# Hashed attention and two gated layers: the order of the first loads, zero matmuls on TensorE at the start, and new due times

## The chip, the cores and the metric

The kernel runs on one core of one Trainium2 chip. What counts is the time of one execution on the device in microseconds (us), the median of several runs. The five engines work side by side: PE (TensorE, matmuls; its weight loads are PEld), DVE (VectorE), ACT (ScalarE), POOL (GpSimd), and SP (SyncE), which here issues most of the loads. ACT and POOL can issue loads too.

## The reference

The inputs are q, k and v of shape (2, 8, 768, 64). Six projections give each query and each key a bucket, and a query sees only the keys of its own bucket:

```python
q_bits = (np.einsum('bhsd,dk->bhsk', q, proj) > 0)
...
mask = q_bucket[:, :, :, None] == k_bucket[:, :, None, :]
scores = np.where(mask, scale * np.matmul(q, k.transpose(0, 1, 3, 2)), -1e9)
attn = softmax(scores)
x = (attn @ v), heads side by side: 1536 tokens x 512
h = x @ w_in;  x = (h - tanh(h)) @ w_out
g = x @ w_gate;  x = (g * sigmoid(g) * (x @ w_val)) @ w_out2
```

## The kernel before

The work is attention over 8 pairs of heads, then the two layers over three blocks of 512 tokens. A pair has 12 steps: two halves of the queries, two heads (e = 0 and 1), three blocks of 128 queries. A step (`declare_step`) computes the scores on PE (L438, into one of two PSUM tiles `s_t`), their maximum on DVE (L447), the exp on ACT (L449), divides by the sum (L453, L455 and, on POOL, L456), transposes on PE (L467) and copies to SBUF (L473). After each half `declare_pv` multiplies with v in two parts (L493). The mask is built into the score matmuls: `prep` and `prep_first` hash q and k (L405 and L363), take the signs as bits on DVE (L346), turn them to one-hot sums on PE (L340), and write the operands on ACT, POOL and DVE (L305, L307, L316, L320, L331, L334). `prep_first` does so for pair 0, head by head, from its own loads; for later pairs `prep(n)` uses a tile y that holds q and k of both heads, and loads q and k once more in the layout of the operands.

Nothing is put in order by hand. Each piece of work is declared with `op`: the engines that may do it and how long it takes there, what it reads and writes, a due time, and a time `after` which it may begin. `Plan.order` then runs a list scheduler over these figures: whenever an engine is free, it takes the ready piece with the earliest due time. The result is one order of all pieces. The kernel emits the instructions in this order, each on its engine, and on the chip each engine works its own queue off in that order, waiting only for data and buffers. The figures themselves (durations, `lat`, `slow`, `after`) don't exist on the chip. The table `DUE` holds the offsets that make the due times: `qk` for scores, `tr` for transposes, `pv` and `pv2` for the two parts with v, `mx`, `ex`, `nm`, `cp` for a step's other pieces, `alt` for the second engine where two may do a piece.

Of the kernel before, what the change touches and what calls it, by code (L numbers as in the profile page):

```python
# [10 lines left out]
BF16 = mybir.dt.bfloat16  # L11
# [23 lines left out]
PVB = 3  # L35
NGS = 21
LAG = 1


def chunk_keys():  # L40
# [8 lines left out]
def chunks():  # L49
# [7 lines left out]


DUE = dict(
    pace=2.46, t0=10.5, qk=-13.61, mx=-13.71, ex=10.42, rc=-7.09, nm=-4.48, tr=-11.45, cp=-19.4, alt=-0.38,  # L60
    pv=29.1, pv2=16.93, xh=36.08, xl=19.15, hash=-8.93, bits=-88.0, oh=-8.61, ohs=8.26, pk=7.49, he=19.64,
    ki=-17.93, kl=-2.38, ko=-26.19, qi=8.99, ql=35.3, qb=-9.42, qo=17.11,
)


class Plan:
# [13 lines left out]
    def op(self, eng, fn, r=(), w=(), due=0.0, lat=None, late=False, after=0.0):  # L80
        n = len(self.ops)
        deps = set()
        for k in r:
            deps.update(self.writers.get(k, ()))
        for k in w:
            deps.update(self.writers.get(k, ()))
            deps.update(self.readers.get(k, ()))
        for k in r:
            self.readers.setdefault(k, []).append(n)
        for k in w:  # L90
            if k in r:
                self.writers.setdefault(k, []).append(n)
            else:
                self.writers[k] = [n]
                self.readers[k] = []
        deps.discard(n)
        self.ops.append((dict(eng), fn, deps, due, self.LAT if lat is None else lat, late, after))
# [75 lines left out]
def lsh_attention_moe_kernel(ctx: ExitStack, tc: tile.TileContext, qT, kT, vP, proj, cst, wts, out):  # L173
    nc = tc.nc
    eng = {"PE": nc.tensor, "DVE": nc.vector, "ACT": nc.scalar, "POOL": nc.gpsimd, "SP": nc.sync}
    const = ctx.enter_context(tc.tile_pool(name="const", bufs=1))
    plan = Plan()
    op = plan.op

    def tiles(stack, name, n, shape, dtype=F32, **kw):  # L180
        pool = stack.enter_context(tc.tile_pool(name=name + "_p", bufs=n, **kw))
        return [pool.tile(shape, dtype, tag=name, name=name) for _ in range(n)]
# [19 lines left out]
    s_t = tiles(ctx, "s", 2, [128, 2, 512], space=PSUM)  # L202
# [7 lines left out]
    def ring(name, n):  # L210

        c = counts[name] = counts.get(name, -1) + 1
        return name, c % n
# [42 lines left out]
    v_t = tiles(at, "v", 2, [128, NKT, 128])  # L256
# [13 lines left out]
    def due_at(step):  # L270
        return T0 + PACE * step

    def load(n, side, e, slow=0.0):
        src, t, nm = ((qT, ldq_t, "q"), (kT, ldk_t, "k"))[side]
        k = ring("ld" + nm, 2)
        r0 = (2 * n + e) * 64
        due = due_at(12 * (n - 1) + (2, -1)[side] + 3 * e)
        for i in range(2):
            op({("SP", "ACT")[side == 0 and n == 0]: 0.55},
               lambda g, i=i: g.dma_start(out=t[k[1]][64 * i:64 * i + 64, :], in_=src[r0:r0 + 64, :]),  # L280
               w=[k + (i,)], due=due if n else -5, lat=3.0 + slow)
        return t[k[1]], [k + (0,), k + (1,)]
# [56 lines left out]
    def oh_mm(ps, pk, side, half, bt, btk, due):  # L339
        op({"PE": 0.165}, lambda g: g.matmul(out=ps, lhsT=pw[:, 2 * side + half, :], rhs=bt, start=True, stop=True),  # L340
           r=[btk, "pw"], w=[pk], due=due, lat=0.25)

    def bits_of(ps, pk, due):
        k = ring("bits", 2)
        t = bit_t[k[1]]
        op({"DVE": 0.47}, lambda g: g.tensor_scalar(out=t, in0=ps, scalar1=0.0, scalar2=None, op0=ALU.is_gt),  # L346
           r=[pk], w=[k], due=due)
        return t, k

    def prep_first():  # L350

        lds = {}
        for e in range(2):
            for side in (1, 0):
                lds[e, side] = load(0, side, e, slow=0.3 + 0.9 * e)
        for e in range(2):
            r = slice(64 * e, 64 * e + 64)
            due = due_at(3 * e)
            bank, hk = ((h_t[0], ("h", 0)), (x_t[0], ("x", 0)))[e]

            def hash_head(g, bank=bank, e=e, r=r):
                for j in range(4):
                    g.matmul(  # L363
                        out=bank[32 * j:32 * j + 32, 0:TB], lhsT=pj[r, :],
                        rhs=lds[e, j // 2][0][r, (j % 2) * TB:(j % 2 + 1) * TB],
                        start=True, stop=True, tile_position=(64 * e, 32 * j),
                    )

            op({"PE": 1.45}, hash_head, r=["pj", *lds[e, 0][1], *lds[e, 1][1]], w=[hk], due=(-60.0, due_at(0))[e], lat=0.25)
            bt, btk = bits_of(bank[:, 0:TB], hk, (-60.0, due_at(0))[e])  # L370
            if e == 0:
                sk = ring("s", 2)
                where = {
                    (1, 0): (s_t[sk[1]][:, 0, 0:TB], sk + (0,)), (1, 1): (s_t[sk[1]][:, 1, 0:TB], sk + (1,)),
                    (0, 0): (t_t[0][:, 0, 0:TB], ("t", 0)), (0, 1): (t_t[0][:, 1, 0:TB], ("t", 1)),
                }
            else:
                where = {
                    (1, 0): (t_t[0][:, 0, 0:TB], ("t", 0)), (1, 1): (t_t[0][:, 1, 0:TB], ("t", 1)),
                    (0, 0): (h_t[0][:, 0:TB], ("h", 0)), (0, 1): (x_t[0][:, 0:TB], ("x", 0)),  # L380
                }
            for i, (side, half) in enumerate(((0, 0), (1, 0), (1, 1), (0, 1))):
                ps, pk = where[side, half]
                dd = (-40.0, due_at(1))[e] + 0.2 * i if i < 3 else due_at(4 + 3 * e)
                oh_mm(ps, pk, side, half, bt, btk, (-50.0, due_at(0))[e] + 0.2 * i)
                (prep_k if side else prep_q)(0, e, half, *lds[e, side], ps, pk, dd)

    def load_y(n):
        for side, src in ((0, qT), (1, kT)):
            op({"SP": 0.4}, lambda g, side=side, src=src: g.dma_start(  # L390
                out=y_t[0][:, side, :], in_=src[n * 128:(n + 1) * 128, :]
            ), w=[("y", side)], due=due_at(12 * (n - 1) - 5), lat=4.0)

    def prep(n):
        base = due_at(12 * n)
# [79 lines left out]

    def load_v(n):
        k = v_k[n] = ring("v", 2)
        op({"SP": 0.4}, lambda g: g.dma_start(out=v_t[k[1]], in_=vP[n]), w=[k], due=due_at(12 * n - 3), lat=3.5)

    def declare_pv(n, half):  # L480
        b_, p_ = pairs[n]
# [97 lines left out]
    def a2(g, tb, j):  # L579
        d, ps, skk = a_mm(2, g, tb, 2 * j)  # L580
        u, uk, u1 = u_slot()
        u = u[:, 0:MB]
        op({"ACT": 0.61}, lambda e: e.activation(out=u, in_=ps[:, 0, :], func=ACTF.Sigmoid), r=skk, w=[uk] + u1, due=d + 0.3)  # L583

        def both(e):
            e.tensor_tensor(out=u, in0=ps[:, 0, :], in1=u, op=ALU.mult)  # L586
            e.tensor_tensor(out=u, in0=ps[:, 1, :], in1=u, op=ALU.mult)  # L587

        op({"DVE": 1.38}, both, r=skk + [uk], w=[uk], due=d + 0.9)
        split_g((2, g, tb, j), u, [uk], d + 2.3)  # L590
# [74 lines left out]
    warm = const.tile([128, 1], F32, name="warm")  # L665
    op({"POOL": 0.1}, lambda g: g.memset(warm, 0.0), w=["warm"], due=-100)
    op({"ACT": 1.5}, lambda g: g.activation(out=warm, in_=warm, func=ACTF.Exp), r=["warm"], w=["warm"], due=-3)
    prep_first()
    load_v(0)
    for i in range(nst):  # L670
        n, r = divmod(i, 12)
        declare_step(i)
        if r % 6 == 5:
            declare_pv(n, r // 6)
        if r == 11 and n + 1 < len(pairs):
            prep(n + 1)
            load_v(n + 1)
# [3 lines left out]
    units += [(2, g, tb) for g in range(NG2) for tb in range(NMB)]  # L681
    for n, (layer, g, tb) in enumerate(units + [(0, 0, 0)] * LAG):
        if layer == 2 and g == 0:
# [4 lines left out]
        elif layer == 2:  # L688
            for j in range(G2):
                a2(g, tb, j)  # L690
        if n >= LAG:
            layer, g, tb = units[n - LAG]
            b(layer, g, tb, ((0, 2), (2, 1), (3, 1)))
# [69 lines left out]
```

## Time and profile before

| | |
|---|---|
| time, median of 3 runs | 811.65 us (811.37 to 811.76) |
| the profiled execution | 811.49 us, span of its instructions 809.6 us |
| PE busy | 782.6 us, 97% of the span |
| DVE, ACT, POOL busy | 503.8, 336.3, 382.5 us |
| HBM read | 57.04 MB |

The span runs from the first to the last instruction; the time adds what lies around it. The page of the profile gives the busy time of each engine; the views of the trace that are shown below give it by stretch, instruction by instruction, and with what each waited for.

### The profile page before, as it was taken

The numbers are of one execution on the slowest core, as the hardware profiler recorded it, in microseconds if no ns is written. First come the engines' busy times: TensorE is split into PE (matmuls) and PEld (weight loads), VectorE is DVE, ScalarE is ACT, GpSimd is POOL, SyncE is SP. The second block draws the span as 40 slices with busy tenths as digits, with TensorE's granted clock in tenths as the row PEclk, the third lists the DMA queues.
The fourth block names the chain that finished last, engine by engine and source line by source line (L and its number), as shares of the span: only waits on it lengthen the run. The fifth ranks groups of instructions, "written<-read, shape, count | busy, mean of one in ns | idle before, by whom it ended". The sixth has DMA issues, their size and how long they took to land.

```text
span 809.6 us, 10578 instructions
## 1 busy us (share of the span) xinstructions
PE 782.6 (97%) x3900; PEld 616.3 (76%) x3900; DVE 503.8 (62%) x734; ACT 336.3 (42%) x583; POOL 382.5 (47%) x387
## 2 busy tenths in 40 slices
PE   4899999999999999999999999999999999999998
PEld 2666676666667788888888888888888888888886
DVE  5988787887788497655556359273725646343223
ACT  4877777787674433322222233333222312211110
POOL 3877766766465564533534367353422423231110
PEclk9999999999999999999999999999999999999999
DMA  7453242230214144212113022020402121000012
GB/s 219 124 146 95 70 127 89 79 98 1 73 53 135 55 141 139 79 35 95 53 53 104 27 79 79 26 84 30 147 1 79 55 101 58 20 1 1 1 52 104
DMA packets 20003, 60.86 MB, mean 75 GB/s; under 512 B 2768, under 2 KB 2768, under 8 KB 19952
## 3 DMA queue, kind: packets, MB, share of 16 engines
q1 hardware_dynamic: 19440, 59.25, 22.8%
q10 hardware_dynamic: 464, 0.80, 0.4%
q8 instruction: 31, 0.51, 0.3%
q0 software_dynamic: 48, 0.13, 0.1%
q14 instruction: 20, 0.16, 0.1%
HBM read 57.04 MB, written 3.15 MB: 74 GB/s over the span
## 4 chain that ended last, share of the span: by engine, by line
PE 86%; ACT 5%; DVE 3%; POOL 2%; issue 2%; DMA 1%; ACTq 0%; POOLq 0%
PE s L536 40%; PE t L619 14%; PE h L619 7%; PE x L619 7%; PE x L493 6%; PE t L467 6%; PE s L438 5%; ACT p L449 3%; DVE m L447 2%; POOL p L456 1%; DMA q<-in_qT 1%; ACT pt L473 1%; POOL op L307 1%; ACT op L334 0%; DVE xl L501 0%
## 5 line engine op out<-in xcount | busy, mean ns | idle before, releaser
L545 POOL TENSOR_TENSOR op<-p,op 128x512 fp32r<-128x512 f32 x84 | 115.9, 1390 | 182.2 <-ACT op L544 173.7
L536 PE MATMUL s<-xh,wb 128*128 128x512 f32 x528 | 165.5, 389 | 0.0
L536 PE MATMUL s<-xh,wa 128*128 128x512 f32 x432 | 136.4, 390 | 0.0
L536 PEld LDWEIGHTS s<-xh,wb 128*128 128x128 f32 x528 | 99.1, 188 | 20.6
L456 POOL TENSOR_SCALAR p<-p,r 128x768 f32<-128x768 f32 x96 | 95.2, 997 | 30.7 <-DVE r L455 29.5
L447 DVE TENSOR_REDUCE m<-s 128x1 f32<-128x768 f32 x96 | 89.0, 951 | 22.7 <-PE s L438 22.1
L536 PE MATMUL s<-xl,wb 128*128 128x512 f32 x264 | 102.7, 389 | 0.0
L438 PE MATMUL s<-op 128*128 128x384 f32 x384 | 85.9, 358 | 9.5 <-ACT p L449 9.0
L536 PEld LDWEIGHTS s<-xh,wa 128*128 128x128 f32 x432 | 81.1, 188 | 17.4 <-issue 0.6
L244 POOL TENSOR_TENSOR wb<-f,wb 128x512 fp32r<-128x512 f32 x38 | 52.7, 1393 | 84.6 <-ACT wb L242 73.9
L449 ACT ACTIVATE p<-s,m 128x768 f32<-128x768 f32 x96 | 85.8, 897 | 12.5 <-DVE m L447 10.0
L586 DVE TENSOR_TENSOR p<-s,p 128x512 f32<-128x512 f32 x36 | 24.8, 690 | 104.6 <-ACT p L583 104.6
L467 PEld LDWEIGHTS t<-csb,p 128*128 128x128 f32 x576 | 64.8, 141 | 29.4 <-issue 17.1
L467 PE MATMUL t<-csb,p 128*128 128x128 f32 x576 | 80.7, 276 | 4.4 <-ACT pt L473 2.6
L544 ACT ACTIVATE op<-p 128x512 fp32r<-128x512 f32 x84 | 50.7, 628 | 81.8 <-DVE p L587 50.4
L536 PE MATMUL s<-xl,wa 128*128 128x512 f32 x216 | 84.1, 389 | 0.0
L583 ACT ACTIVATE p<-s 128x512 f32<-128x512 f32 x36 | 21.6, 599 | 139.5 <-PE s L536 138.0
L438 PEld LDWEIGHTS s<-op 128*128 128x128 f32 x384 | 65.1, 191 | 18.6 <-ACT p L449 17.2
L233 DVE TENSOR_SCALAR f<-raw 128x512 uint32<-128x512 uint32 x68 | 54.2, 797 | 33.6 <-POOL wb L244 13.4
L236 DVE SCALAR_TENSOR_TENSOR f<-raw,f 128x512 uint32<-128x512 uint32 x68 | 72.3, 1064 | 1.4
L239 DVE SCALAR_TENSOR_TENSOR f<-raw,f 128x512 uint32<-128x512 uint32 x68 | 69.7, 1026 | 1.0
L493 PE MATMUL x<-pt,v 128*64 128x384 f32 x384 | 68.8, 494 | 0.0
(91 smaller groups left out, 1124.4 us busy)
## 6 DMA issues: line engine op xcount, KB each, us to landing
raw<-in_w SPq DMA_DIRECT2D x68, 512.0 KB, 3.3
k<-in_kT SPq DMA_DIRECT2D x32, 192.0 KB, 3.1
q<-in_qT SPq DMA_DIRECT2D x28, 192.0 KB, 3.6
v<-in_v SPq DMA_DIRECT2D x8, 384.0 KB, 3.5
y<-in_qT SPq DMA_DIRECT2D x7, 384.0 KB, 3.1
y<-in_kT SPq DMA_DIRECT2D x7, 384.0 KB, 4.0
out<-acc SPq DMA_DIRECT2D x3, 512.0 KB, 2.8
out<-acc SPq DMA_DIRECT2D x6, 256.0 KB, 2.1
```

The source lines that it names most:

```text
L233: op({"DVE": 0.6}, lambda e: e.tensor_scalar(out=f, in0=hi32, scalar1=3, scalar2=0x3FFFFFF8, op0=ALU.logical_shift_left, op1=ALU.bitwise_a ...
L236: op({"DVE": 0.95}, lambda e: e.scalar_tensor_tensor(out=f, in0=lo32, scalar=29, in1=f, op0=ALU.logical_shift_right, op1=ALU.bitwise_or), ...
L239: op({"DVE": 0.95}, lambda e: e.scalar_tensor_tensor(out=f, in0=hi32, scalar=0xC0000000, in1=f, op0=ALU.bitwise_and, op1=ALU.bitwise_or), ...
L438: g.matmul(out=s[:, kh, 0:TB], lhsT=(b, a)[first][:, q0], rhs=ks[kh][0 if first else 1], start=first, stop=not first,)
L447: op({"DVE": 0.87}, lambda g: g.tensor_reduce(out=m, in_=sv, axis=AX.XY, op=ALU.max, negate=True), r=[sk + (0,), sk + (1,)], w=[mk], due=d ...
L449: op({"ACT": 0.9}, lambda g: g.activation(out=p.rearrange("p (a b) -> p a b", a=2), in_=sv, func=ACTF.Exp, bias=m, accum_out=sm), r=[sk + ...
L456: op({"POOL": 0.95}, lambda g: g.tensor_scalar(out=p, in0=p, scalar1=r, scalar2=1.0, op0=ALU.mult, op1=ALU.mult), r=[pk, rk], w=[pk], due= ...
L467: g.transpose(out=t_t[0][:, kt // 3, c0:c0 + 128], in_=p[:, kt * 128:(kt + 1) * 128], identity=ident)
L493: g.matmul(out=x[r, :], lhsT=v[:, kt, r], rhs=pt_t[ptks[e][1]][:, kt, :], start=(kt == 0), stop=(kt == NKT - 1), tile_position=(0, 64 * e),)
L536: g.matmul(out=ps, lhsT=w[:, wi, kt * 128:(kt + 1) * 128], rhs=(xh_a, xl_a)[xi][:, kt, tb * MB:(tb + 1) * MB], start=(n == 0), stop=(n == ...
L545: op({"POOL": 1.4}, lambda g: g.tensor_tensor(out=lo, in0=src, in1=hi.bitcast(F32), op=ALU.subtract), r=srck + [hk], w=[lk] + l1, due=due ...
L619: e.matmul(out=o, lhsT=l, rhs=r, start=(n == 0), stop=(n == 3 * ng - 1))
```

## The change

Three things change. The loads of y for every pair may begin in the planner's order only after 5.5, v of pair 0 after 8.0 and v of the other pairs after 16.0, and the planner takes the loads of pair 0 to land later (`slow`). A tile `rest` of zeros is written by DVE, and 66 matmuls multiply it with itself (128 x 128 by 128 x 256, bf16) into the first bank of `s_t[1]`; each may begin in the planner's order at a time of its own and is due at 20.0. And all of `DUE` has new values.

```diff
+WARM = 66
...
 DUE = dict(
-    pace=2.46, t0=10.5, qk=-13.61, mx=-13.71, ex=10.42, rc=-7.09, nm=-4.48, tr=-11.45, cp=-19.4, alt=-0.38,
-    pv=29.1, pv2=16.93, xh=36.08, xl=19.15, hash=-8.93, bits=-88.0, oh=-8.61, ohs=8.26, pk=7.49, he=19.64,
-    ki=-17.93, kl=-2.38, ko=-26.19, qi=8.99, ql=35.3, qb=-9.42, qo=17.11,
+    pace=2.4, t0=13.38, qk=4.32, mx=-25.84, ex=12.05, rc=-10.2, nm=-13.2, tr=-26.1, cp=30.59, alt=-14.51,
+    pv=-7.5, pv2=23.62, xh=36.69, xl=-27.55, hash=-12.04, bits=-92.94, oh=-12.35, ohs=5.39, pk=48.56,
+    he=13.11, ki=-7.49, kl=-9.87, ko=-53.97, qi=-5.84, ql=75.72, qb=19.68, qo=7.53,
 )
...
-                lds[e, side] = load(0, side, e, slow=0.3 + 0.9 * e)
+                lds[e, side] = load(0, side, e, slow=0.4 + 1.2 * e)
...
-            ), w=[("y", side)], due=due_at(12 * (n - 1) - 5), lat=4.0)
+            ), w=[("y", side)], due=due_at(12 * (n - 1) - 5), lat=4.0, after=5.5)
...
-        op({"SP": 0.4}, lambda g: g.dma_start(out=v_t[k[1]], in_=vP[n]), w=[k], due=due_at(12 * n - 3), lat=3.5)
+        op({"SP": 0.4}, lambda g: g.dma_start(out=v_t[k[1]], in_=vP[n]), w=[k], due=due_at(12 * n - 3), lat=3.5, after=(8.0, 16.0)[n > 0])
...
+    rest = const.tile([128, 256], BF16, name="rest")
+    op({"DVE": 0.2}, lambda g: g.memset(rest, 0.0), w=["rest"], due=-100)
+    for i in range(WARM):
+        tm = 0.9 + 0.213 * i if i < 18 else 0.9 + 0.213 * 18 + 0.12 * (i - 18)
+        op({"PE": 0.2 if i < 18 else 0.107}, lambda g: g.matmul(
+            out=s_t[1][:, 0, 0:256], lhsT=rest[:, 0:128], rhs=rest, start=True, stop=True,
+        ), r=["rest"], w=[("s", 1, 0)], due=20.0, lat=0.0, after=tm)
     prep_first()
```

## Rows read from the trace of the kernel before

**Rows 1.** The page, part 1: busy time, share of the span, instructions.
```profile
PE 782.6 (97%) x3900; PEld 616.3 (76%) x3900; DVE 503.8 (62%) x734; ACT 336.3 (42%) x583; POOL 382.5 (47%) x387
```
**Rows 2.** Busy time by stretch at the start, and all attention: length, engines, granted clock.
```profile
17.06:36.50 19.44, 15.06 (x91) 10.87 (x92) 17.98 (x34) 17.79 (x35) 16.97 (x25) 1.00 0.51 148
...
14.40:241.50 227.10, 213.12 (x1372) 150.63 (x1371) 187.43 (x370) 173.48 (x331) 153.83 (x214) 1.00 0.30 89
0.00:10.50 10.50, 1.50 (x8) 0.23 (x8) 3.22 (x8) 3.08 (x6) 2.58 (x10) 1.00 0.81 198
10.50:17.06 6.56, 6.49 (x27) 3.52 (x31) 5.36 (x9) 2.39 (x6) 2.61 (x4) 1.00 0.78 259
```
**Rows 3.** The same view: one attention pair in steady state, and the layers.
```profile
158.40:187.20 28.80, 27.56 (x182) 19.41 (x180) 23.00 (x48) 22.48 (x43) 19.58 (x28) 1.00 0.28 83
...
278.00:540.00 262.00, 262.00 (x1158) 216.94 (x1157) 166.30 (x173) 84.05 (x124) 130.30 (x91) 1.00 0.23 75
```
**Rows 4.** The chain of waits, start to 45 us: start us, us, what.
```profile
0.73 2.35 DMA pj<-in_proj
...
3.11 7.36 DMA q<-in_qT
...
10.51 1.50 PE x L363 x8
...
14.09 2.56 PE s L438 x8
...
39.46 1.39 PE s L438 x8
```
**Rows 5.** Timeline of PE: start us, us, instruction, idle before it and its releaser.
```profile
11.95 0.50 PE L340 MATMUL t<-bits,pw 128*128 128x384 bf16 x1
12.24 0.85 PE L340 MATMUL s<-bits,pw 128*128 128x384 bf16 x2
...
16.98 0.85 PE L405 MATMUL h<-y,pj 128*32 128x384 f32 x8
...
21.52 0.45 PE L438 MATMUL s<-op 128*128 128x384 f32 x1 [0.58 <-ACT op L334]
...
25.87 0.97 PE L438 MATMUL s<-op 128*128 128x384 f32 x4 [0.40 <-ACT p L449]
...
36.50 2.16 PE L493 MATMUL x<-pt,v 128*64 128x384 f32 x12
```
**Rows 6.** DMA view of four short stretches: issues with us to landing, bytes, rates.
```profile
k<-in_kT SPq DMA_DIRECT2D x1, 192.0 KB, 3.2
...
q<-in_qT ACTq DMA_DIRECT2D x1, 192.0 KB, 3.9
...
q1 hardware_dynamic: 437, 1.14, 42.5%
...
DMA packets 224, 0.60 MB, mean 397 GB/s; under 512 B 30, under 2 KB 30, under 8 KB 224
```
**Rows 7.** Timeline of SP's queue: the loads in the order of their issue.
```profile
3.95 0.35 SPq L390 DMA_DIRECT2D y<-in_qT  x1
5.06 0.34 SPq L390 DMA_DIRECT2D y<-in_kT  x1
6.31 1.72 SPq L478 DMA_DIRECT2D v<-in_v  x2
8.61 7.91 SPq L280 DMA_DIRECT2D k<-in_kT  x4
```
**Rows 8.** Timeline of DVE, POOL and ACT between 13 and 19 us.
```profile
13.02 0.54 DVE L346 TENSOR_SCALAR bits<-x 128x384 bf16<-128x384 f32 x1
...
16.25 0.51 POOL L307 TENSOR_SCALAR op<-k 128x384 fp32r<-128x384 f32 x1 [3.65 <-DMA k<-in_kT]
...
16.93 0.58 ACT L334 ACTIVATE op<-t,csb 64x384 fp32r<-64x384 f32 x1 [2.76 <-PE t L340]
...
18.07 0.90 ACT L449 ACTIVATE p<-s,m 128x768 f32<-128x768 f32 x1
```
**Rows 9.** Waits of PE in one pair, 158.4 to 187.2: us in total, times, longest.
```profile
PE s L438 <- ACT p L449: 0.8, 2, 0.6
PE t L467 <- ACT pt L473: 0.3, 1, 0.3
```

## The prediction

> **What bounds the kernel now.** I read the page's busy times first: TensorE (PE) works 97% of the span, so only its idle time can be won [rows 1]. Then the busy time by stretch, to see where it idles. From 278 us on there is nothing to win: 262.00 of 262.00 us are busy. An attention pair in its steady state leaves 28.80 - 27.56 = 1.24 us, the whole stretch from 14.4 to 241.5 us leaves 227.10 - 213.12 = 13.98, and 17.06 to 36.50 alone leaves 19.44 - 15.06 = 4.38 of these [rows 2, 3]. The first 10.5 us hold 1.50 us of work. Third, the chain of waits over the start: PE waits for the last q load of head 1 (landed at 10.47), hashes it in 1.50 us, and runs the eight score matmuls of steps 0 and 1 from 14.09 to 16.65 [rows 4]. So the end of the kernel moves by what PE's idle time changes, and the change can reach three places: before 17 us, 17 to 36 us, and the holes in the steady state.
>
> In 17.06 to 36.50 the other engines are nearly full: DVE 17.98, ACT 17.79, POOL 16.97 of 19.44 us [rows 2]. PE's 4.38 us there are waits for them, not for the start itself.
>
> **The clock.** The column of the granted clock says 1.00 in every stretch, but the same eight score matmuls take 2.56 us at 14.09 and 1.39 us at 39.46 [rows 2, 4]. 2.56 / 8 = 0.32 us for 384 columns is the 1.2 GHz level, 1.39 / 8 = 0.174 us is near the 2.4 GHz level. Eight hash matmuls take 1.50 us at 10.51 and 0.85 us at 16.98 [rows 4, 5]: PE rose to the upper level somewhere before 16.98, after steady work since 10.51. A zero matmul has 256 columns and no row; scaled by columns it is 0.213 us at the lower level and 0.116 us at the upper one.
>
> **The loads.** `after` only moves an instruction in the planner's order; no engine waits for that time. What makes loads wait on the chip is something else: the last q load is issued at 3.11, when pj has landed; the first y at 3.95, when the first k load has (0.73 + 3.2); the second y at 5.06, when the first q load has (1.14 + 3.9) [rows 4, 6, 7]. Each goes when the load eight places before it has landed. In the new order SP still has nothing but y to issue after its four k loads (pair 1's k loads need slots that are read first), so y keeps its place and its 3.95 and 5.06, and v of pair 0 its 6.31. Only v of pair 1 moves, behind the first loads of pair 1. Cost or gain for the q load at 10.47: nothing, because v was queued behind y anyway. But pair 1's k comes sooner: POOL waited 3.65 us for it until 16.25 [rows 8]. The 384 KB of the moved v at the 397 GB/s of that stretch are 1.0 us [rows 6]. POOL stands in the chain after 18 us, so this is worth 0 to 1.0; the other engines are as full as POOL, and I take half, -0.5. The moved v has its first reader far later: even pair 0's first v matmul starts at 36.50 [rows 5].
>
> **The zero matmuls.** There are 66, due at 20.0, each writing the first bank of `s_t[1]`. Step 0 writes the same bank, so all 66 stand ahead of step 0 in PE's queue. I worked the order out by hand from the planner's rules (its durations serve for the order alone): 20 of them, the hash of head 0, 8 more, the hash of head 1, four one-hot matmuls, 10 zero matmuls, three one-hots, 28 zero matmuls, step 0. The planner expects head 1's load at 7.2 (issued from 2.05 to 2.60, and 3.0 + 1.6 more); the trace has it at 10.47 [rows 4]. So 28 zero matmuls fill the wait, and 38 run after it, when PE has real work.
>
> Step by step at the upper clock. The first 20 end near 5.2 even at 0.213 each from about 0.95 (the queues begin at 0.73 [rows 4], then the memset on DVE, which is busy for 3.22 of the first 10.5 us [rows 2]); head 0's q lands at 1.14 + 3.9 = 5.04 [rows 6]: 0.2 us at most, hidden by the wait for head 1. The 8 end by about 7, in time that was idle: nothing. Hash of head 1 from 10.51, 0.85 us: 11.36. Four one-hots, 0.17 each (half of what the pair at 12.24 adds to one at the lower level, 0.85 - 0.50) [rows 5]: 12.04. Ten zero matmuls, 1.16: 13.2. The next one-hots need the bits of head 1, which DVE finishes at 13.56 behind the work that waits for the same load [rows 8]: 13.6 + 0.51 = 14.1. Twenty-eight zero matmuls, 3.25: 17.35. Steps 0 and 1, 1.4: 18.75, against 16.65. So the first scores come 2.1 us later, although every matmul is faster. Without the 28 zero matmuls it would be 15.5.
>
> What of the 2.1 us reaches the end? Behind step 0 stand its maximum on DVE, its exp on ACT, and so step 2. Before, the exp of step 0 started only at 18.07, although the scores were there by then, because ACT stood 2.76 us at L334 for a one-hot that PE ran after the scores [rows 8]; in the new order the one-hots come first. New: scores of step 0 at 18.05, maximum 0.96, exp at 19.1, 1.0 us late. Step 3 lost another 0.58 us to L334 before (at 21.52), which goes too [rows 5]. DVE, the fullest engine, has the same preparation done by then, in another order. So the delay shrinks step by step, and I expect step 5 (25.87 before) level: 0, with ends of -1.8 (all of ACT's 2.76 us won, less the 1.0) and +2.1.
>
> At this place a page bears on the sum. The trace shows the lower level at 14.09 after PE had idled until 10.51 [rows 4]. The Trainium skill, "TensorE: Matmul & The Clock Gate", section "Why this matters for your kernels", says that idle gaps between bursts put the clock back to half. By that rule the wait from about 7 us to 10.5 undoes the warming, and the delay would be the one of the second rival below; no run here shows a gap after warming.
>
> **The new due times.** They reorder all of attention. Before, both v parts had the last place on PE (29.1 behind their step) and ran whenever nothing else was ready; now part 0 comes early (-7.5), part 1 23.62 later, and transposes go ahead of scores (-26.1 against 4.32). The steady holes are waits for exp, 0.8 us, and for a copy, 0.3 us, in each pair [rows 9]: PE has run out of ready work. A part kept back can fill one. Some six pairs with 0.8 us are 4.8 us; I take half, -2.4, since the planner fills only what it sees, and its landing times differ from the chip's. Bounds: all idle time after 36.5 us gone would be -(13.98 - 4.38) = -9.6; on the other side a v block of 2.16 us [rows 5] ahead of ready scores, which starves ACT, could double the waits for exp: +4.8.
>
> **Sum.** The profiled execution took 811.49 us: span 809.6 and 1.9 around it; the median of the runs is 811.65, 0.16 above. 811.5 + 0 - 0.5 - 2.4 = 808.6.
>
> **Rivals.**
> *No net change:* the new priorities only move the holes. For it: PE is at 27.56 of 28.80 us in pair after pair, little slack to find [rows 3]. 811.5 - 0.5 = 811.0.
> *The zero matmuls cost what they take:* 38 of them stand behind the load, the 2.1 us are not made up by step 5, and no holes are filled. Place: PE between 11.4 and 17.4 us. 811.5 + 2.1 - 0.5 = 813.1, about the edge to slower; with the clock back at the lower level until about 16.5, as before, hash 12.0, one-hots 13.3, zero matmuls 15.4, one-hots 16.4, zero matmuls at the upper level 19.7, scores 21.1: +4.4, or 815.4. It decides once step 5 starts more than 1.6 us after 25.87. Against it: PE's idle 4.38 us in the next 20 us can take it in.
> *v first starves ACT:* +4.8 - 0.5, 815.8. Against it: ACT and DVE have 22.48 and 23.00 us of work in 28.80, so they can catch up [rows 3].
> *Holding back works after all:* if y left SP only after q had landed, the 0.35 MB of it that moved before 10.5 (1.14 MB on that queue less four k loads of 192 KB) would clear the way by 0.9 us at 397 GB/s [rows 6]: 807.7. Against it: the order argument above.
>
> **Numbers.** A difference within 0.2% (1.6 us: 810.0 to 813.3) is what a measurement of this kernel can't tell from no change. Chances: forecast 0.42, holding back works 0.05, no net change 0.26, zero matmuls 0.16 (half of it near 813, half with the lower clock), v first 0.11. Faster takes 0.47 and 0.01 of no net change, 0.48; slower 0.11 and 0.13 of the zero matmuls, 0.24; the same what is left of these two, 0.28. The range reaches from 804.8 (forecast with three quarters of the bound of 9.6 won) to 815.4, and leaves some 2 in 10 out. The forecast's own range is 805 to 810.
>
> **What would show it.** Right: y issued near 3.95 and 5.06 as now; zero matmuls between the hash of head 1 and step 0; step 0 near 17.4; step 5 near 25.9; less than 1.24 us idle in a pair. Wrong: head 1's load well before 10.4, step 0 by 14, or PE waiting more than 1.1 us a pair for exp and copies. The forecast falls most easily at the due times: their term is the largest and the least supported by rows.

## The result, and the profile after

The changed kernel takes 819.97 us, the median of four runs (818.53 to 821.25), against 811.51 on the same chips. The ratio is 1.0106, 95% interval 1.0094 to 1.0118: slower by some 8.5 us, outside the range. One execution of each of two experiments took 22 and 38% longer at a granted clock of 0.75 and 0.66, and is left out of the times below. In the profiled execution (819.18 us) the span grew from 809.6 to 817.4 us. Line numbers of the code shown in the rows are one higher than before.

Page, part 1, PE's own entry leads the line:

```profile
PE 791.6 (97%) x3966; PEld 622.2 (76%) x3966; DVE 515.1 (63%) x742; ACT 336.9 (41%) x581; POOL 373.0 (46%) x382
```

PE is 9.0 us busier than in [rows 1], for a span 7.8 us longer: it idles 1.2 us less. So the kernel is not slower because PE waits more in total, but because the waiting it lost was filled with 66 matmuls that compute nothing, and new waiting came in elsewhere. Busy time by stretch (length, then PE, PEld, DVE, ACT, POOL, granted clock, DMA share, GB/s):

```profile
10.50:17.06 6.56, 5.80 (x26) 2.69 (x27) 4.07 (x8) 2.59 (x6) 2.58 (x4) 0.52 0.60 200
0.00:10.50 10.50, 5.60 (x36) 3.48 (x36) 2.83 (x8) 2.83 (x5) 2.81 (x9) 1.00 0.81 190
17.06:36.50 19.44, 16.05 (x107) 12.53 (x106) 18.31 (x32) 15.11 (x31) 12.80 (x20) 0.99 0.63 183
158.40:187.20 28.80, 27.42 (x180) 19.04 (x179) 24.34 (x49) 22.74 (x44) 17.68 (x27) 1.00 0.26 83
278.00:540.00 262.00, 262.00 (x1161) 216.01 (x1158) 161.01 (x167) 83.70 (x124) 131.46 (x92) 1.00 0.22 73
```

Against [rows 2, 3]: the layers are as full as before; a steady pair leaves 1.38 us idle instead of 1.24; and the granted clock between 10.50 and 17.06 is 0.52, the 1.2 GHz level, after 28 zero matmuls had run and PE had stood. The chain of waits over the start answers to [rows 4]:

```profile
3.00 8.22 DMA q<-in_qT
...
11.26 1.51 PE x L364 x8
...
14.16 2.13 PE s L673 x10
...
17.25 2.10 PE s L673 x17
...
19.52 1.20 PE s L673 x11
20.72 0.72 PE s L439 x4
```

The zero matmuls (L673) are themselves in the chain: 2.13 + 2.10 + 1.20 = 5.43 us between the hash of head 1 and the first scores. The first ten run at 0.21 us each, the last eleven at 0.11. Head 1's q landed at 11.22 (3.00 + 8.22), 0.75 us later than before. PE's timeline, answering to [rows 5]:

```profile
11.26 0.85 PE L364 MATMUL x<-q,pj 64*32 64x384 f32 x2 [4.26 <-DMA q<-in_qT]
...
20.48 1.66 PE L439 MATMUL s<-op 128*128 128x384 f32 x8
...
27.88 1.66 PE L439 MATMUL s<-op 128*128 128x384 f32 x8
...
67.96 0.97 PE L439 MATMUL s<-op 128*128 128x384 f32 x4 [0.64 <-ACT p L450]
```

Steps 0 and 1 have their scores at 22.1 us, not 16.65; step 5 starts at about 28.6 (second half of the group at 27.88), 2.7 us late, beyond the 1.6 us at which the prediction said its rival would be decided; step 21, the first clean mark in pair 1, starts at 67.96 against 61.78 before. The same view of the kernel before, steps 0 and 1, 6 and 21:

```profile
13.64 3.01 PE L438 MATMUL s<-op 128*128 128x384 f32 x8
...
27.49 0.96 PE L438 MATMUL s<-op 128*128 128x384 f32 x4
...
61.78 0.97 PE L438 MATMUL s<-op 128*128 128x384 f32 x4 [0.62 <-ACT p L449]
```

SP's queue, against [rows 7]:

```profile
4.02 0.35 SPq L391 DMA_DIRECT2D y<-in_qT  x1
5.05 0.34 SPq L391 DMA_DIRECT2D y<-in_kT  x1
7.61 0.33 SPq L479 DMA_DIRECT2D v<-in_v  x1
8.30 8.61 SPq L281 DMA_DIRECT2D k<-in_kT  x4
...
22.07 0.58 SPq L479 DMA_DIRECT2D v<-in_v  x1
```

Both y loads go where they went; v of pair 0 goes 1.3 us later (6.31 before), and v of pair 1 has moved behind pair 1's k and q loads. Further on, y of pair 2 goes at 22.94 instead of 17.86, right after the late hash of pair 1's y (L406, at 22.06 instead of 16.98). Waits of PE in the pair from 158.4 to 187.2, against [rows 9]:

```profile
PE s L439 <- ACT p L450: 1.0, 2, 0.7
PE t L468 <- ACT pt L474: 0.3, 1, 0.3
```

### The profile page after: what moved, and what is told of

Same layout as the page of the kernel before. It is cut to its first block, busy times and chain, and to the rows that moved or that the text cites. A ratio compares the mean times of both kernels' runs of the same rounds, so it can differ in the third digit from the quotient of the medians.

```text
span 817.4 us, 10704 instructions
## 1 busy us (share of the span) xinstructions
PE 791.6 (97%) x3966; PEld 622.2 (76%) x3966; DVE 515.1 (63%) x742; ACT 336.9 (41%) x581; POOL 373.0 (46%) x382
## 4 chain that ended last, share of the span: by engine, by line
PE 84%; DVE 7%; ACT 3%; issue 2%; POOL 2%; DMA 1%; ACTq 0%; POOLq 0%; DVEq 0%
PE s L537 40%; PE t L620 14%; PE h L620 7%; PE x L620 7%; PE x L494 5%; PE t L468 5%; PE s L439 5%; DVE m L448 2%; ACT p L450 2%; DVE op L321 1%; DVE op L317 1%; DMA q<-in_qT 1%; PE s L673 1%; ACT op L335 1%; POOL op L332 1%
## 5 line engine op out<-in xcount | busy, mean ns | idle before, releaser
L234 DVE TENSOR_SCALAR f<-raw 128x512 uint32<-128x512 uint32 x68 | 56.1, 825 | 34.9 <-POOL wa L245 13.7
L237 DVE SCALAR_TENSOR_TENSOR f<-raw,f 128x512 uint32<-128x512 uint32 x68 | 70.5, 1036 | 1.5
L240 DVE SCALAR_TENSOR_TENSOR f<-raw,f 128x512 uint32<-128x512 uint32 x68 | 68.9, 1015 | 1.0
```

What stands on the lines that cost most here:

```text
L234: op({"DVE": 0.6}, lambda e: e.tensor_scalar(out=f, in0=hi32, scalar1=3, scalar2=0x3FFFFFF8, op0=ALU.logical_shift_left, op1=ALU.bitwise_a ...
L237: op({"DVE": 0.95}, lambda e: e.scalar_tensor_tensor(out=f, in0=lo32, scalar=29, in1=f, op0=ALU.logical_shift_right, op1=ALU.bitwise_or), ...
L240: op({"DVE": 0.95}, lambda e: e.scalar_tensor_tensor(out=f, in0=hi32, scalar=0xC0000000, in1=f, op0=ALU.bitwise_and, op1=ALU.bitwise_or), ...
```

## PE's idle time, stretch by stretch

The view of busy time by stretch gives PE's idle time as length less busy time. The same stretches for the kernel before, the changed one and four of the experiments below (us):

| stretch | before | after | order, no zeros | zeros alone | due times alone | 52 zeros, no gap |
|---|---|---|---|---|---|---|
| 0 to 17.06 | 9.07 | 5.66 | 11.54 | 5.16 | 8.97 | 3.18 |
| 17.06 to 26 | 3.19 | 1.05 | 1.64 | 1.86 | 2.03 | 2.61 |
| 26 to 56 | 1.53 | 4.72 | 3.62 | 2.72 | 4.74 | 2.26 |
| 56 to 72 | 0.92 | 1.05 | 0.94 | 1.04 | 0.93 | 0.93 |
| 72 to 216 | 6.19 | 7.03 | 7.08 | 6.19 | 7.09 | 6.18 |
| 216 to 260 | 2.16 | 2.34 | 2.30 | 2.17 | 2.18 | 2.17 |
| sum | 23.06 | 21.85 | 27.12 | 19.14 | 25.94 | 17.33 |
| PE busy, whole span | 782.6 | 791.6 | 784.1 | 790.4 | 783.6 | 787.5 |
| span | 809.6 | 817.4 | 815.2 | 813.5 | 813.4 | 808.8 |

From 260 us on PE has no hole in any of them. Two of the rows of this table carry the case. From 26 to 56, where pair 0 hands over to pair 1, PE of the kernel before idles 1.53 of 30 us, and every other kernel of the table idles more. And each version with the new due times has 0.84 to 0.90 us more from 72 to 216. The stretches are fixed in time, though, while a late kernel is at earlier work in them: the zero matmuls alone have the order of before, and their 2.72 us come from the shift. So the stretch from the scores of step 6 to those of step 21 is compared as well. It takes 34.29 us with 2.14 idle before, 34.22 with 2.15 for the zeros alone, 36.84 with 3.46 for the changed kernel, the same with 3.47 for its order without zeros, and 37.68 with 5.38 for the due times alone. In the changed kernel PE also does 1.2 us more of other work in it. The rows themselves, of the kernel before and then of the changed one:

```profile
26.00:56.00 30.00, 28.47 (x184) 20.48 (x184) 27.84 (x52) 23.51 (x46) 25.67 (x39) 1.00 0.38 107
72.00:216.00 144.00, 137.81 (x902) 97.06 (x900) 114.37 (x233) 110.59 (x211) 92.79 (x130) 1.00 0.28 85
27.49:61.78 34.29, 32.15 (x206) 22.68 (x204) 31.34 (x59) 27.34 (x54) 28.43 (x42) 1.00 0.37 108
```

```profile
26.00:56.00 30.00, 25.28 (x161) 18.14 (x161) 29.29 (x52) 20.83 (x42) 22.33 (x36) 1.00 0.38 112
72.00:216.00 144.00, 136.97 (x892) 95.49 (x888) 121.50 (x237) 113.13 (x213) 87.23 (x127) 1.00 0.27 85
31.12:67.96 36.84, 33.38 (x212) 23.01 (x212) 33.34 (x59) 25.87 (x51) 26.36 (x40) 1.00 0.30 87
```

## The experiments

The first theory was the rival of the zero matmuls (called the queue theory in the expectations): what they delay at the start stays. Its rival was that the new due times make the loss (due theory). Sixteen kernels ran; each ratio is to runs of the kernel before on the same chip.

### The parts apart

**The planned order without zero matmuls** (the planner still counts them; none is issued):

```diff
-        op({"PE": 0.2 if i < 18 else 0.107}, lambda g: g.matmul(
+        op({"PE": 0.2 if i < 18 else 0.107}, lambda g, i=i: i < 0 and g.matmul(
```

> The changed kernel with its planned order kept, instruction for instruction, but none of the 66 zero matmuls issued (their result is read by nobody). Queue theory: the 38 zero matmuls behind the hash of head 1 hold step 0 back by 2.13 + 2.1 + 1.2 = 5.4 us and this is not made up; without them the scores of steps 0 and 1 run at the lower clock again (+1.1), so 819.97 - 5.4 + 1.1 = 815.7 us. Due-time theory: the loss comes from the new order of attention behind the start, so 819 to 820. Load theory: head 1's q lands 0.75 us later because of the new order of the loads: landing stays at 11.2 and the time near 819.

Measured 817.12 us, ratio 1.0073 (1.0057 to 1.0090). So the zero matmuls themselves account for 2.9 of the loss, and 5.6 lie in the order of the rest. PE's timeline:

```profile
17.36 3.01 PE L439 MATMUL s<-op 128*128 128x384 f32 x8
...
25.67 1.64 PE L439 MATMUL s<-op 128*128 128x384 f32 x8
...
65.75 0.97 PE L439 MATMUL s<-op 128*128 128x384 f32 x4 [0.64 <-ACT p L450]
```

Without zeros the first scores still come late, at 17.36, at the lower clock (3.01 us, as before, for what took 1.66 in the changed kernel; the column of the granted clock reads 1.00 there all the same). Step 4 starts at 25.67 instead of 22.58, but step 5, the second half of that group, at about 26.4, only some 0.6 us late. Step 6 (28.91) is 1.4 us late, step 21 is 4.0 late and the end of the span 5.6. So most of the loss arises after step 5. Head 1's q landed at 10.83 here, so nothing supports the load theory, by which the new order of the loads would hold it at 11.2.

**Only the 28 zero matmuls before head 1's hash**:

```diff
-        op({"PE": 0.2 if i < 18 else 0.107}, lambda g: g.matmul(
+        op({"PE": 0.2 if i < 18 else 0.107}, lambda g, i=i: i < 28 and g.matmul(
```

> The changed kernel with its planned order kept, but only the first 28 zero matmuls issued, those ahead of the hash of head 1. Queue theory: as without any, 815.7 us, because PE still idles some 4 us before the hash of head 1 and the clock falls back, so the 28 cost and give nothing. If the 28 do keep the clock up: 1.5 - 0.85 = 0.65 us on the hash, 0.6 on the one-hots and 1.1 on the scores earlier, 813.3. Due-time theory: 819 to 820.

Measured 817.17 us, 1.0077 (1.0062 to 1.0092): the same as with none. The granted clock was 0.55 from 10.5 to 17.06. Warming that ended in a gap of 4.0 us gave nothing here.

**The zero matmuls alone**, in the order of before:

```diff
@@ prep_first, ahead of the hash of head e
+                zeros(g, (20, 8)[e])
@@ declare_step, ahead of the scores
+            if i == 0:
+                zeros(g, 38)
```

> The kernel before with its own order, due times and loads, and the 66 zero matmuls at the changed kernel's three places: 20 ahead of the hash of head 0, 8 behind it, 38 directly ahead of step 0. Queue theory: from 13.6 some 16 zero matmuls at 0.213 us, then 22 at 0.116, so step 0 at 19.6 and the scores of steps 0 and 1 done at 21.0 against 16.65: +4.4, 815.9 us. Due-time theory: PE's idle time between 17 and 36 us takes the delay in, 811.5 to 812.5. Load theory: no change, 811.5.

Measured 815.70 us, 1.0056 (1.0041 to 1.0071). PE's timeline:

```profile
14.61 4.74 PE L676 MATMUL s<-rest 128*128 128x256 bf16 x38
19.10 1.64 PE L441 MATMUL s<-op 128*128 128x384 f32 x8
...
29.91 0.96 PE L441 MATMUL s<-op 128*128 128x384 f32 x4 [0.40 <-ACT p L452]
...
65.74 0.97 PE L441 MATMUL s<-op 128*128 128x384 f32 x4 [0.64 <-ACT p L452]
```

Step 5 is 4.04 us late, step 21 is 3.96 late, the kernel is 4.1 longer. With the order kept, nothing of a delay at the start is made up. In this trace head 1's q landed at 11.19 instead of 10.47, so some 0.7 of the 4.04 us were there before the zero matmuls behind the hash began.

**The new due times alone**, the whole table `DUE` of the change and nothing else:

```diff
-    pace=2.46, t0=10.5, qk=-13.61, mx=-13.71, ex=10.42, rc=-7.09, nm=-4.48, tr=-11.45, cp=-19.4, alt=-0.38,
+    pace=2.4, t0=13.38, qk=4.32, mx=-25.84, ex=12.05, rc=-10.2, nm=-13.2, tr=-26.1, cp=30.59, alt=-14.51,
...
```

> The kernel before with the new due times and nothing else of the change: no zero matmuls, no times for the loads. Queue theory: only the 0.23 us that a pair in steady state has lost (29.07 against 28.84), seven times: +1.6, 813.1 us. Due-time theory: the whole loss, 818 to 820. Load theory: 811.5 to 813.

Measured 815.65 us, 1.0055 (1.0040 to 1.0071), between the two theories. The start is good (step 0 at 14.18, step 5 at 25.17); step 21 comes at 64.26, 2.5 late, and the rest is lost in the later pairs. PE's longest wait of the hand-over, and in the chain the load behind it:

```profile
47.78 0.33 PE L340 MATMUL h<-bits,pw 128*128 128x384 bf16 x1
49.84 0.98 PE L438 MATMUL s<-op 128*128 128x384 f32 x4 [1.73 <-ACT p L449]
```

```profile
40.09 5.82 DMA q<-in_qT
...
46.07 0.52 POOL op L307
...
46.61 0.56 DVE op L316
```

Operand work of pair 2 now stands in POOL's and DVE's queues ahead of pair 1's steps. It waits for a load issued at 40.09 that lands at 45.91, and the steps behind it wait too.

**The loads alone, as the planner sees them**:

```diff
-                lds[e, side] = load(0, side, e, slow=0.3 + 0.9 * e)
+                lds[e, side] = load(0, side, e, slow=0.4 + 1.2 * e)
...
-            ), w=[("y", side)], due=due_at(12 * (n - 1) - 5), lat=4.0)
+            ), w=[("y", side)], due=due_at(12 * (n - 1) - 5), lat=4.0, after=5.5)
...
-        op({"SP": 0.4}, lambda g: g.dma_start(out=v_t[k[1]], in_=vP[n]), w=[k], due=due_at(12 * n - 3), lat=3.5)
+        op({"SP": 0.4}, lambda g: g.dma_start(out=v_t[k[1]], in_=vP[n]), w=[k], due=due_at(12 * n - 3), lat=3.5, after=(8.0, 16.0)[n > 0])
```

> The kernel before with the change of the loads alone (later beginnings for y and v in the planner, later landings assumed), old due times, no zero matmuls. Order argument: y goes out at 3.95 and 5.06 as before, head 1's q lands at 10.4, and what differs is only what the planner rearranges behind it: 811.5 to 813.5. Load theory: head 1's q lands at 11.2 as in the changed kernel, +0.75 and whatever follows: 812.3 or more. If holding back did what its words say: q lands near 9.6 and 810.6.

Measured 816.60 us, 1.0068 (1.0055 to 1.0081). The y loads were issued at 4.01 and 4.90, and head 1's q landed at 10.37: on the chip's loads before 10 us the edit does nothing but move v of pair 1 (to 21.03). But the planner, told that loads come later, put other work first everywhere; PE was busy 135.97 of the 144 us from 72 to 216, 1.84 less than before.

**The one load that moves**, v of pair 1 put behind pair 1's k and q loads, the rest as before:

```diff
+    v1 = next(o for o in order if o[0] == v_op[1])
+    i, j = order.index(v1), max(k for k, o in enumerate(order) if o[0] in q_op)
...
+    order[i:j + 1] = order[i + 1:j + 1] + [v1]
```

> The kernel before with one load moved: v of pair 1 goes behind the k and q loads of pair 1 on SP, everything else in its old order. This is all that the held-back loads change in SP's queue at the beginning. By my forecast pair 1's k lands up to 1.0 us earlier and POOL's wait until 16.25 shrinks: 811.0 (0 to 1.0 gained). If the loads themselves cost the 5.1 us that the planner's version of them cost: 816.6. If nothing hangs on it: 811.5.

Measured 811.60 us, 0.9999 (0.9990 to 1.0008): nothing, although pair 1's k reached POOL at 15.26, 1.0 us sooner.

**Loads held back for real**: both y(1) loads and v of pairs 0 and 1 are issued by ACT, behind head 1's first q operand, so that they can't start before that load has landed (`held` keeps what SP no longer issues).

```diff
+        def first(g):
+            scaled(g, a, src, 0.125)
+            if (n, e, half) == (0, 1, 0):
...
+                for fn in held[1:3] + held[:1] + held[3:]:
+                    fn(g)
+
+        op(scale(n), first, r=lk, w=[ak_ + (0,), ak_ + (1,)], due=due + lag(n, "qi"))
```

> The kernel before with y of pair 1 and v of pairs 0 and 1 really held back: ACT issues the four loads itself, right behind its first operand of head 1's q, so none of them can move before that q has landed. If the 0.35 MB of y that moved before 10.5 delayed q: it lands 0.9 us earlier, near 9.6, and the time is 810.6 us. If not: 10.4 and 811.5. A later y (needed at 16.98) costs at most what its landing after 17 takes, some 0.5.

Measured 812.05 us, 1.0009 (1.0001 to 1.0018). Head 1's q landed at 10.78, no earlier than with y in front of it (10.47; over all these kernels the landing spreads by 1.1 us), and the time has none of the 0.9 us. The rival "holding back works after all" falls, even with the loads really held.

### Zero matmuls where PE only waits

**20 before head 0's hash and 32 before head 1's, order of before**:

```diff
+                zeros(g, (20, 32)[e])
```

> The kernel before with 52 zero matmuls, 20 ahead of head 0's hash and 32 behind it, all ahead of head 1's hash, order and due times as before. The run with 60 gave 0.7 us, where 2.2 were possible; its last zero matmuls may have run past the landing. If that was it: 32 end before 10.4 in any case, the hash and the first scores run at the upper clock, 809.5 us. If the clock drops in the short gap that is left, or the engines behind take the gain away: 810.8 to 811.5.

Measured 810.98 us, 0.9995 (0.9986 to 1.0004). PE's timeline:

```profile
6.66 3.67 PE L674 MATMUL s<-rest 128*128 128x256 bf16 x32
10.70 0.51 PE L364 MATMUL x<-q,pj 64*32 64x384 f32 x2 [0.36 <-DMA q<-in_qT]
...
13.24 1.69 PE L439 MATMUL s<-op 128*128 128x384 f32 x8
...
24.55 0.97 PE L439 MATMUL s<-op 128*128 128x384 f32 x4 [0.40 <-ACT p L450]
```

With 0.36 us idle instead of 4.26 the clock is kept: the scores of steps 0 and 1 take 1.69 us against 3.01 before (at 13.64, shown above). Step 5 is 1.3 us early, step 21 only 0.76 (61.02). What PE gains, it waits for ACT and POOL later: 2.26 us idle from 26 to 56 instead of 1.53. So here an early start shrank on the way, and a late one didn't.

**20 and 40** in the same places:

```diff
+                zeros(g, (20, 40)[e])
```

> The kernel before with its own order, and 60 zero matmuls, all ahead of head 1's hash: 20 before the hash of head 0, 40 behind it, none before step 0. If PE kept at work over the wait stays at the upper clock: hash of head 1 0.65 us shorter, one-hots 0.5, scores of steps 0 and 1 1.1, so these scores are done 2.2 us earlier, and since a delay at this place has come through to the end whole, a gain should too: 809.3 us. If the clock doesn't hold, or the engines behind set the pace after all: 811.5. If 40 overrun the landing at 10.47: up to 812.

Measured 810.80 us, 0.9991 (0.9983 to 1.0000): no more than the 32. Both lie within the 0.2% that a measurement of this kernel can't tell from no change.

### What the planned order loses between step 5 and step 21

**Scores of steps 0 and 1 ahead of head 1's one-hots** on PE, in the order with 28 zeros (817.17 us):

```diff
+    moved = [o for o in order if o[0] in early_qk]
...
+    order = [o for o in order if o[0] not in early_qk]
+    at_ = min(i for i, o in enumerate(order) if o[0] in one_hots)
+    order[at_:at_] = moved
```

> The changed kernel's planned order with the first 28 zero matmuls, and one thing moved: the scores of steps 0 and 1 stand ahead of head 1's one-hots on PE, as in the kernel before. Start theory: the 4.0 us by which the run without zero matmuls was late at step 21 came from step 0 standing behind those one-hots, so what stays is the 1.6 us of the later pairs, 813.2 us. If the place of step 0 is not the cause: 817.

Measured 819.28 us, 1.0097 (1.0082 to 1.0112). The scores were done at 16.69, but DVE took the maximum of step 0 only at 20.98, behind head 1's operands in its queue; PE waited 3.05 us for that exp, steps 2 and 3 came at 23.01 (in 2.93 us, at a granted clock of 0.50) and step 21 at 67.83.

**The same with maximum and exp moved as well**:

```diff
+        if i < 2:
+            early_qk += [len(plan.ops), len(plan.ops) + 1]
```

> The changed kernel's planned order with the first 28 zero matmuls, and scores, maximum and exp of steps 0 and 1 all moved ahead of head 1's one-hots, on PE, DVE and ACT. Queue-order theory: with the scores alone moved, DVE still took the maximum of step 0 at 20.98, behind all of head 1's preparation, because the zero matmuls had held step 0 back in the plan of every engine; with all three moved, exp of step 0 comes near 16.5 to 18, step 21 near 62 to 63.5, and the 1.6 us of the later pairs stay: 813 to 814.5. If the order further on is what costs: 816 to 817.

Measured 820.50 us, 1.0113 (1.0099 to 1.0126). The exps ran at 16.41 and 17.73 as wanted. Now head 1's one-hots waited for DVE, the transposes of step 0 waited 3.16 us for POOL, and in the gaps the granted clock fell to 0.74 over 17 to 36.5. So moving step 0 gave nothing back, twice; but both edits brought waits and a lower clock of their own.

**Copies of steps 5 to 8 back to ACT.** From 26 to 56 DVE is busy 29.3 of 30 us in the order without zeros, and the new due times give it these four copies of 0.95 us, which before were ACT's. In that order (`copy_op` notes the copy of each step):

```diff
+    given = {copy_op[i]: e for e, ii in (("ACT", (5, 6, 7, 8)),) for i in ii}
+    order = [(n, given.get(n, e), t) for n, e, t in order]
```

> The new order without its zero matmuls (817.12 us), with one thing changed by hand: the copies of the transposed tile in steps 5, 6, 7 and 8 go to ACT, as in the kernel before, and not to DVE. DVE theory (DVE, busy 29.3 of the 30 us from 26 to 56, sets the pace of steps 5 to 16, and the four copies of 0.95 us are its surplus over the order before): 813.0 to 814.5 us, step 21 at 62 to 63 (from 65.75). Order theory (the loss lies in the sequence of the work as a whole, on whichever engine the copies are): 816.5 to 817.5 us, step 21 where it was.

Measured 816.69 us, 1.0073 (1.0060 to 1.0085): 0.4 back of 817.12, which the intervals don't tell from nothing. DVE fell to 25.94 us, and PE idled 3.25 us in the stretch instead of 3.62. From step 6 to step 21 it took 36.25 us instead of 36.84. A full DVE looked like the bound and held 0.6 us of it at most. Between 17 and 72 us PE's waits for DVE's copies fell from 1.8 to 0.8 us, and those for POOL's normalisation, the exp and ACT's copies rose from 4.0 to 5.5.

**The same four copies to DVE in the kernel before**:

```diff
+    given = {copy_op[i]: e for e, ii in (("DVE", (5, 6, 7, 8)),) for i in ii}
```

> The kernel before with the copies of steps 5 to 8 given to DVE, as the new due times give them, and nothing else of the change. DVE theory: DVE has 2.2 us left from 26 to 56 before and takes 3.8 more, so 813.0 to 815.5 us. Order theory: 811.3 to 812.3 us.

Measured 816.88 us, 1.0066 (1.0053 to 1.0079): 5.4 us for four copies that change engine. PE's timeline, then the stretches around it:

```profile
42.43 0.85 PE L469 MATMUL t<-csb,p 128*128 128x128 f32 x6 [1.67 <-DVE pt L476]
...
46.33 1.47 PE L469 MATMUL t<-csb,p 128*128 128x128 f32 x6 [2.27 <-DVE pt L476]
47.45 1.63 PE L440 MATMUL s<-op 128*128 128x384 f32 x4
```

```profile
46.00:48.00 2.00, 1.67 (x8) 1.70 (x9) 0.81 (x3) 0.42 (x2) 1.21 (x3) 0.60 0.97 286
48.00:50.00 2.00, 2.00 (x8) 1.69 (x7) 1.61 (x2) 0.54 (x1) 0.00 (x0) 0.55 0.84 187
50.00:52.00 2.00, 2.00 (x17) 1.26 (x17) 1.84 (x4) 1.96 (x6) 1.39 (x2) 1.00 0.10 34
```

PE waits for copies, and after the second of those waits it runs at the lower clock for some 4 us. Six transposes take 1.47 us instead of 0.85, four scores 1.63 instead of 0.97.

**New due times alone, copies of steps 4, 6, 7 and 8 to ACT**:

```diff
+    given = {copy_op[i]: e for e, ii in (("ACT", (4, 6, 7, 8)),) for i in ii}
```

> The kernel before with the new due times alone (815.65 us), the copies of steps 4, 6, 7 and 8 given to ACT. DVE has 4.7 us left from 26 to 56 there, and its worst wait, 2 us before step 15, is for a load of pair 2 that lands at 45.91. DVE theory gives up to 1.5 us back (814.2 to 815.0); if the hand-over from pair 0 to pair 1 costs by that load, nothing (815.3 to 816.0).

Measured 815.48 us, 1.0048 (1.0035 to 1.0062): nothing back, as the rival of the late load has it; that load was not moved itself.

### The later pairs

**New due times alone, the low part of every k operand on POOL** for pairs 1 to 7, since DVE has 121 us of work from 72 to 216 there and 114 before:

```diff
+        if n:
+            k_low.append(len(plan.ops))
...
+    order = [(n, "POOL" if n in k_low else e, t) for n, e, t in order]
```

> The kernel with the new due times alone, its planned order kept, but every low part of k (L331, pairs 1 to 7) given to POOL, where the planner had put half of them on DVE. If DVE's extra work (121.05 against 114.37 us in five pairs) is what makes the later pairs slower: 815.65 - 1.3 = 814.3 us. If not: 815.7, or more where POOL's 1.0 us for one comes later than DVE's.

Measured 819.42 us, 1.0099 (1.0085 to 1.0113). DVE fell to 113.90 us, and PE to 133.67, 3.2 us worse. One low part takes POOL 1.0 us or more and DVE 0.6 to 0.7, so this shows that giving the work to POOL doesn't help, not that DVE's extra work costs nothing.

**New due times alone, the copy of step 8 of pairs 1 to 6 on DVE**, as before:

```diff
+    given = {copy_op[i]: e for e, ii in (("DVE", (20, 32, 44, 56, 68, 80)),) for i in ii}
```

> The new due times alone (815.65 us), with the copies of step 8 of pairs 1 to 6 given to DVE, as before; the new due times give them to ACT, on whose exponentials PE waits 1.0 us a pair there against 0.8 before. If ACT's extra copy is what makes a later pair 0.2 us longer: 814.2 to 814.8 us, 72 to 216 with PE busy 137.5 and more. If it is not: 815.4 to 816.2.

Measured 818.31 us, 1.0091 (1.0075 to 1.0106): 2.7 us worse, PE at 134.50. Taking the extra copy off ACT gives nothing back either. Here one wait of 1.83 us in the hand-over was followed by the lower clock, by stretch:

```profile
48.00:50.00 2.00, 0.25 (x2) 0.00 (x0) 2.00 (x4) 0.96 (x3) 1.87 (x3) 1.00 0.00 0
50.00:52.00 2.00, 1.92 (x7) 1.82 (x8) 1.36 (x3) 1.94 (x5) 0.41 (x2) 0.55 0.00 0
```

## Why the prediction was wrong

**The loads: right on the chip, wrong in the sum.** Both y loads, the moved v and the order of the queue came as read from the rows [rows 6, 7]; v of pair 0 came 1.3 us later than the 6.31 it was given. Pair 1's k came 0.5 us sooner, as argued, and it was worth nothing: the term of -0.5 is 0.0 (with v alone moved, k came 1.0 us sooner). The sentence that `after` only moves an instruction in the planner's order was taken too narrowly: it was priced for the loads, while the planner rearranged everything else around their later landing times. That alone costs 5.1 us, and the sum had no term for it.

**The zero matmuls: the step "I expect step 5 level" failed.** The hand-worked order of PE was right but for one one-hot, which runs between the last zero matmuls. Two of the step's conditions were not. It was worked at the upper clock, and PE stood 4.26 us after the 28, so hash, one-hots and the first ten zero matmuls ran at the lower level. That is the variant of the second rival with the lower clock: its times for hash, one-hots, zero matmuls and scores are 0.8 to 1.0 us early throughout, 0.75 of it by the later landing of head 1's q. The Trainium skill, "TensorE: Matmul & The Clock Gate", section "Why this matters for your kernels", says that idle gaps between bursts put the clock back to half; the trace agrees (granted 0.52 after, 0.55 with the 28 alone, and upper level when only 0.36 us are left idle). And the delay of the scores was to be taken in by PE's idle 4.38 us behind it. Those are waits for engines whose work hangs on the same scores, so they move with them: the zeros alone delay step 5 by 4.04 us and the end by 4.1. The rival's 815.4 was within 0.3 of that kernel, in part by luck: it holds -0.5 for the loads, which that kernel doesn't have, and no later landing. Within the whole change the zero matmuls account for 2.9 us; the new order starts its scores late anyway (17.36 without them).

**The due times: the sign was wrong.** "A part kept back can fill one" gave -2.4; alone they cost 4.1 us. Of the idle time after 26 us that was to be filled, the changed kernel has 15.14 us against 10.80 before (the table's four last stretches). Compared step by step, the due times alone leave 5.38 us idle from step 6 to step 21 against 2.14, where pair 0 hands over to pair 1, and 7.37 against 6.49 in the 154.2 us behind it. The waits for exp and copies in a pair went from 1.1 to 1.3 us, beyond the 1.1 that the prediction named as its refutation. The rival "v first starves ACT" has the size (815.8) but not the place: PE's waits for the exp were to double from 0.8 us a pair, and are 1.0. "No net change" (811.0) falls as well. None of the rivals had the hand-over as its place. The prediction read one steady pair and the start, and not the 30 us between, where the other three engines together are busier than in any later stretch of the table (23.5 to 27.8 us of work each). That any piece put first by the planner delays a step there is my reading; only the late load and the four copies on DVE show it.

**The range.** Its lower end was mis-added: the forecast with three quarters of 9.6 won is 811.5 - 0.5 - 7.2 = 803.8, not 804.8. Nothing hangs on it, since the miss is at the other end.

**Put together.** 2.9 for the zero matmuls and, by subtraction, 5.6 for the planned order are the measured 8.5. The parts alone (4.1, 4.1 and 5.1) don't add to it; the planner makes another order from each set of inputs.

**Open.** The planned order without zeros is some 0.6 us late at step 5, 4.0 at step 21 and 5.6 at the end, and no single piece was found that holds what is lost on the way. A late load explains it for the due times alone, where the trace shows the wait, but wasn't taken out by an experiment. A full DVE (0.4 us back for four copies) is excluded as the whole cause; moving step 0 was worse both times, by what the moves themselves brought, so its place isn't excluded as a part. Why a later pair is 0.1 to 0.2 us longer is open as well: the two pieces that were moved made it worse. Head 1's q landed between 10.2 and 11.3 us over these kernels, three times at 11.1 to 11.3 without any zero matmul; what sets it wasn't found, and starts in single traces differ by that much.

## What to carry to other kernels

When an order comes out of a list scheduler, any edit of its inputs is a new order: price first a stretch in which all engines are nearly full at once, for in the one here every new order of the table lost. Idle time right behind a delayed piece of work is no reserve if it waits for results of that piece. Filler matmuls kept the clock only where they ran up to the moment PE's work arrived, and even there the gain was within the noise; those that stood in the queue behind that moment delayed all that followed.

## What the runs showed of the hardware

**A short wait can cost the clock in mid-kernel.** With the four copies on DVE, two waits of PE of 1.67 and 2.27 us, and with the copy of step 8 on DVE, one of 1.83 us, were followed by stretches at a granted clock of 0.55 to 0.60 (shown above). So were a wait of 2.35 us with the copies of steps 4, 6, 7 and 8 on ACT, and one of 1.77 us with the low part of k on POOL (0.50 from 30 to 32). Waits of 1.73 us with the due times alone (46 to 56 reads 1.00), of 1.71 us in the changed kernel (27 to 29 reads 1.00) and of 2.19 us in the order without zeros, copies to ACT, were not. The stretches after 2.35 us, then after 2.19 us:

```profile
33.00:35.00 2.00, 2.00 (x9) 1.91 (x8) 1.24 (x4) 1.98 (x4) 1.79 (x2) 0.50 0.05 12
```

```profile
26.00:28.00 2.00, 1.77 (x13) 1.77 (x14) 1.44 (x2) 1.14 (x3) 1.78 (x4) 1.00 1.06 324
```

The length of the wait alone doesn't decide it in these rows; what does isn't shown. So a stall's price was its length, or its length and more: for the two groups shown with the copies on DVE, 0.62 + 0.66 = 1.3 us.

**DVE's operand op waits out a POOL op.** The scalar-tensor-tensor op of `op` (L317) takes 0.56 us alone. In the changed kernel it more often meets a POOL normalisation that has already begun; DVE first, then POOL:

```profile
130.94 1.21 DVE L317 SCALAR_TENSOR_TENSOR op<-q,op 64x384 fp32r<-64x384 f32 x1
```

```profile
129.96 1.79 POOL L457 TENSOR_SCALAR p<-p,r 128x768 f32<-128x768 f32 x2
```

POOL ends at 131.75, DVE 0.40 us after it, at 132.15. Between 100 and 210 us the median of this op is 0.764 us, 0.555 before. The Trainium skill, "SBUF — State Buffer", section "🔬 SBUF: two separate sides", says that a VectorE op with two SBUF inputs and a GpSimd op that reads SBUF exclude each other for the whole instruction; the trace agrees in so far as DVE's op ended behind POOL's, though the 0.40 us between them are less than its 0.56 alone. Taking other work off DVE didn't make the kernel measurably faster, so this isn't shown to cost time here.
